# Attention and feed-forward on one core: the value products of chunks 3 to 11 in quarters of the array, in two phases

## The chip, the cores and the metric

The kernel runs on one core of one Trainium2 chip. The metric is the device time of one execution in microseconds (us), median of several runs. Engines are named as in the profile: PE is TensorE's matrix product, PEld its weight load, DVE is VectorE, ACT ScalarE, POOL GpSimd, SP SyncE, whose queue issues most transfers.

## The reference, cut to what matters

Attention over 4 batches, 8 heads, 768 positions and a head width of 64, in which each position sees the first 4 keys (sinks) and the last 128; then a feed-forward layer on 3072 rows of 512 with 2048 inner columns. All in float32.

```python
scores = scale * np.matmul(q, k.transpose(0, 1, 3, 2))
is_sink = pos[None, :] < int(n_sink)              # n_sink = 4
rel = pos[:, None] - pos[None, :]
in_window = (rel >= 0) & (rel < int(window))      # window = 128
scores = np.where(is_sink | in_window, scores, -1000000000.0)
a = np.exp(scores - np.max(scores, axis=-1, keepdims=True))
a = a / (np.sum(a, axis=-1, keepdims=True) + 1e-09)
attn_out = np.matmul(a, v)                        # (4, 8, 768, 64)
x = attn_out.transpose(0, 2, 1, 3).reshape(3072, 512)
h = x @ w_in
g = np.maximum(h, 0.0) + alpha * np.minimum(h, 0.0)
return g @ w_out
```

## The kernel before

The 3072 rows are 12 chunks of 256 queries (`QC`), three to a batch (`CPB`). A chunk's 8 heads are 4 pairs `p` (or `x`), two heads `j` each; its 256 queries are two blocks `u` of 128. A block of queries needs two blocks of 128 keys, the older and the newer one; because the window is exactly 128 wide, key place `a` (0 to 127) counts for query `b` in the older block where `a > b` and in the newer one where `b >= a`. So the softmax of the two blocks is added into one tile `comb` (L747), which is turned so that keys lie on partitions, and then multiplied by two triangular masks `tri` (128 x 2 x 128), one for each block. The first chunk of a batch (0, 3, 6, 9) has no older block for its first 128 queries.

In chunks 3 to 11 (`PAIRED` and on) a pair is turned without PE. `swap` (L830) lets DVE transpose 32 x 32 squares into `small`, SP store this to memory (`swap`, L837, one transfer) and load it back in another order (L839, one transfer) into `t`, both `comb` tiles. The masks follow at `trans` (L810): for pairs 0 and 1 `swapped` (L855, the multiplications on L863) writes both masked forms into a `wa` tile; for pairs 2 and 3 `halved` (L843, L850 and L852) writes one into a further `comb` tile and the other in place. There are 5 `comb` and 2 `wa` tiles. `masks_in_order` (L806) puts the rows of `tri` once, ahead of chunk 3, into the order in which the turned keys lie, by a store to `trid` (L807) and a load (L808); the values `v` come in the same order from an input of their own, `vq`.

`av_four` (L950) then multiplies: four full-array products with the sinks (L961) open two PSUM banks, one for pairs 0 and 1, one for pairs 2 and 3. For each pair and each block of keys `blk` follow two products, one for each head `j`, that use all 128 rows (keys) and 64 columns (head width) of the array: head 0 in the left half of the columns, head 1 in the right. Block 1 has 256 columns of queries (it is the newer block for `u` = 0 and the older for `u` = 1), blocks 0 and 2 have 128. Pairs 0 and 1 are issued in `values` (L879), pairs 2 and 3 on L977. ACT (L982) and DVE (L983) split each bank into the two parts `xh` and `xl` that the feed-forward products use: `gemm1` (L997) makes the inner columns, one block of 128 after the other, `gemm2` (L1052 to L1055) the output.

The order on every engine is written by a planner (`Plan`): each operation carries a cost, the planner draws the times from the costs and picks the next operation on every engine, and the program is issued in this order. A changed cost or buffer so moves other operations too. In the scores of chunks 0 and 1 (L675), two heads share the array by rows: 64 rows each, into two banks.

Of the kernel before, what the change touches and what calls it, by code (L numbers as in the profile page):

```python
# [9 lines left out]
F32 = mybir.dt.float32  # L10
# [7 lines left out]
ALU = mybir.AluOpType  # L18

P = 128  # L20
B, H, S, D = 4, 8, 768, 64
# [3 lines left out]
QC = 2 * P  # L25
# [3 lines left out]
CPB = S // QC  # L29
NCHUNK = B * CPB  # L30
NF = DF // P
KT = DM // P
# [56 lines left out]
class Plan:  # L89
# [20 lines left out]
    def held(self, tile_):  # L110
        v = Value(None)
        v.at = tile_
        return v

    def op(self, engine, cost, run, reads=(), writes=(), tail=0.09, mode=None, nbytes=0, other=None, locks=False):
        o = Op(engine, cost, tail, run, self.rank if engine == "PE" else None)
        o.ways = {engine: (cost, run)}
        if other:
            o.ways[other[0]] = other[1:]
        o.born = self.rank  # L120
        if engine == "PE":
# [24 lines left out]
        o.takes = [v for v in seen if v.kind]  # L146
        o.locks = locks
        self.ops.append(o)
        return o
# [161 lines left out]
def dve(n, fast=False):  # L311
    return 0.07 + (0.52e-3 if fast else 1.04e-3) * n
# [22 lines left out]
def mm(n):  # L335
    return 0.456e-3 * n
# [6 lines left out]
def native(n):  # L343
    return 1.667e-3 * n
# [3 lines left out]
ISSUE = 0.45  # L348
# [4 lines left out]
def program(ctx, tc, qk, pairs, vp, vq, vs, w, par, out):  # L353
    nc = tc.nc
# [17 lines left out]
    trid = held(scratch.tile([P, 2, P], F32, name="trid"))  # L372
# [188 lines left out]
    def known(x):  # L561
        return V.setdefault(x, held(x))
# [241 lines left out]
        op("ACT", cast(QC, True), lambda: nc.scalar.copy(st.at, tp.at[:, :QC]), reads=[tp], writes=[st])  # L804

    def masks_in_order():  # L806
        op("SP", ISSUE, lambda: nc.sync.dma_start(trid.at, tri), reads=[known("tri")], writes=[trid], nbytes=8 * P * P)  # L807
        op("SP", ISSUE, lambda: nc.sync.dma_start(tri, trid.at.rearrange("(j a) l x -> a j (l x)", j=4)), reads=[trid], writes=[known("tri")], nbytes=8 * P * P)  # L808

    def trans(c, p):  # L810
        if c in SPLIT:
# [18 lines left out]
    def swap(c, p):  # L830

        cb = comb.pop((c, p))
        small, d, t = val("comb"), val("swap"), val("comb")
        op("DVE", dve(4 * P), lambda: nc.vector.transpose(
            small.at.rearrange("p (j t b) -> p t j b", t=4, j=4), cb.at.rearrange("p (t j b) -> p t j b", t=4, j=4)),
            reads=[(cb, (j, u)) for j in range(2) for u in range(2)], writes=[small])
        op("SP", ISSUE, lambda: nc.sync.dma_start(d.at.rearrange("i (a j) x -> (i a) (j x)", j=4), small.at),  # L837
           reads=[small], writes=[d], nbytes=4 * P * 4 * P)
        op("SP", ISSUE, lambda: nc.sync.dma_start(t.at.rearrange("p (i x) -> p i x", i=4), d.at.rearrange("i p x -> p i x")),  # L839
           reads=[d], writes=[t], nbytes=4 * P * 4 * P)  # L840
        turned[c, p] = t

    def halved(c, p):  # L843

        t, e = turned.pop((c, p)), val("comb")
        at = lambda u: t.at.rearrange("p (i j u b) -> p u i j b", i=4, j=2, u=2)[:, u]
        to = lambda u: e.at.rearrange("p (j u i b) -> p u i j b", i=4, j=2, u=2)[:, u]
        mask = lambda l: tri[:, l].rearrange("p (i b) -> p i b", i=4).unsqueeze(2).broadcast_to([P, 4, 2, 32])
        for u in range(2):
            op("DVE", dve(2 * P), lambda u=u: nc.vector.tensor_tensor(to(u), at(u), mask(u), ALU.mult), reads=[t, known("tri")], writes=[(e, u)])  # L850
        for u in range(2):
            op("DVE", dve(2 * P), lambda u=u: nc.vector.tensor_tensor(at(u), at(u), mask(1 - u), ALU.mult), reads=[known("tri")], writes=[t])  # L852
        wt[c, p] = (t, e)

    def swapped(c, p):  # L855
        if p > 1:
            return halved(c, p)
        t, tt = turned.pop((c, p)), val("wa")
        full = lambda: tt.at.bitcast(F32).rearrange("p (j u l x) -> p j u l x", j=2, u=2, l=2)
        view = lambda: t.at.rearrange("p (i j u b) -> p j u i b", i=4, j=2, u=2)  # L860
        for j in range(2):
            for u in range(2):
                op("DVE", dve(2 * P), lambda j=j, u=u: nc.vector.tensor_tensor(  # L863
                    full()[:, j, u].rearrange("p l (i b) -> p l i b", i=4),
                    view()[:, j, u].unsqueeze(1).broadcast_to([P, 2, 4, 32]),
                    tri.rearrange("p l (i b) -> p l i b", i=4), ALU.mult), reads=[t, known("tri")], writes=[(tt, (j, u))])
        wt[c, p] = tt

    turned = {}

# [10 lines left out]
    def values_cost(c):  # L881
        return native(P) * (4 if c % CPB else 3)
# [31 lines left out]
    def av_split(c, g):  # L914
# [29 lines left out]
        if c and not g:  # L944
# [2 lines left out]
        op("DVE", dve(4 * P), lambda: nc.vector.tensor_tensor(x2.at[:, g], view(), x1.at[:, g].bitcast(F32), ALU.subtract),  # L947
           reads=[rb, *keys[0]], writes=keys[1])

    def av_four(c):  # L950
        every = range(KT)
        kept = [wt.pop((c, x)) for x in every]
        src = [*kept[:2], *kept[2], *kept[3]]
# [5 lines left out]
        def sinks():  # L959
# [4 lines left out]
        def all_values():  # L964
            sinks()
            for x in every:
                if x < 2:
                    values(c, v[x].at, lambda j: kept[x].at.bitcast(F32)[:, j * 4 * P:(j + 1) * 4 * P], place(x), x == 1)
                    continue
                t, e = kept[x]  # L970
                blocks = [(1, lambda j: t.at.rearrange("p (i j u b) -> p j u i b", i=4, j=2, u=2)[:, j], slice(0, 2 * P))]
                if c % CPB:
                    blocks.append((0, lambda j: e.at[:, j * QC:j * QC + P], slice(0, P)))
                blocks.append((2, lambda j: e.at[:, j * QC + P:(j + 1) * QC], slice(P, 2 * P)))
                for n, (blk, what, os) in enumerate(blocks):
                    for j in range(2):
                        nc.tensor.matmul(place(x)[j * D:(j + 1) * D, os], v[x].at[:, blk, j], what(j), start=False, stop=x == KT - 1 and n == len(blocks) - 1)  # L977
        op("PE", 4 * mm(QC) + 4 * values_cost(c), all_values, reads=src + v + [vt, st], writes=bks, tail=N_TAIL, mode="col")
# [205 lines left out]
    n = 0  # L1184
# [250 lines left out]
```

## Time and profile before

| | |
|---|---|
| median of 3 runs | 640.63 us (640.63 to 640.88) |
| profiled execution | 641.19 us, its span 639.6 us |
| PE busy | 630.7 us (99%) |
| PEld, DVE, ACT, POOL busy | 560.6, 522.0, 392.4, 35.2 us |
| granted TensorE clock | 0.999 of full speed |

A profile is of one execution, so its own time stands beside the median. The span runs from the first to the last instruction. PE's busy time joins rows that overlap: a matmul's row lasts until its results are out, while the next one starts earlier.

### The profile page before, as it was taken

The page shows a single profiled execution, that of the slowest core. Times are in us where ns is not written, and L with a number is a line of the kernel's source. Part 1 is how long each engine was busy: PE and PEld are TensorE (multiplying, and loading weights), DVE is VectorE, ACT ScalarE, POOL GpSimd, SP SyncE. Part 2 cuts the span into 40 slices and gives each one's busy share as a digit, 9 for nine tenths or more (in the row PEclk, how much of TensorE's full clock was granted, in tenths as well). Part 3 has the DMA queues.
Part 4 walks back from the last instruction along what each step waited for, and adds up shares of the span by engine and source line. Part 5 has one row for each costly group of instructions (what it writes and reads, how often), then busy time and mean ns, then how long its engine had stood idle before and what let it go on. Part 6 is the DMA issues. An engine that isn't in the chain of part 4 may idle for free. (4 is left out here: it accounts for less than half of the span.)

```text
span 639.6 us, 13100 instructions
## 1 busy us (share of the span) xinstructions
PE 630.7 (99%) x4497; PEld 560.6 (88%) x4497; DVE 522.0 (82%) x1748; ACT 392.4 (61%) x1060; POOL 35.2 (6%) x115
## 2 busy tenths in 40 slices
PE   7999999999999999999999999999999999999997
PEld 3677688979989999999989999999998998998996
DVE  6999999998969988986987997995996997895332
ACT  6998888847638636736637745654755754752332
POOL 2120000000100000000100000000100000000000
PEclk9999999999999999999999999999999999999999
DMA  8676630424344345333443344442543434421001
GB/s 315 251 261 246 240 131 22 126 82 148 110 128 151 104 124 179 92 120 109 158 133 121 128 130 130 129 136 61 165 132 112 150 100 149 130 83 35 34 3 36
DMA packets 58825, 83.08 MB, mean 130 GB/s; under 512 B 9088, under 2 KB 35328, under 8 KB 58752
## 3 DMA queue, kind: packets, MB, share of 16 engines
q1 hardware_dynamic: 55200, 69.20, 33.9%
q10 hardware_dynamic: 3552, 12.98, 5.6%
q8 instruction: 37, 0.61, 0.4%
q14 instruction: 36, 0.29, 0.1%
HBM read 65.12 MB, written 17.04 MB: 128 GB/s over the span
## 5 line engine op out<-in xcount | busy, mean ns | idle before, releaser
L1001 ACT ACTIVATE g<-bank,param 128x256 f32<-128x256 f32 x192 | 90.6, 473 | 85.9 <-PE bank L997 85.4
L997 PE MATMUL bank<-xh,win 128*128 128x256 f32 x768 | 140.0, 278 | 0.0
L997 PE MATMUL bank<-xh,w 128*128 128x256 f32 x768 | 138.9, 276 | 0.0
L997 PEld LDWEIGHTS bank<-xh,w 128*128 128x128 f32 x768 | 121.1, 192 | 1.9 <-issue 0.7
L997 PEld LDWEIGHTS bank<-xh,win 128*128 128x128 f32 x768 | 120.8, 192 | 1.8 <-issue 1.1
L1007 ACT CAST gh<-g 128x256 fp32r<-128x256 f32 x176 | 70.7, 405 | 64.5 <-DVE g L1002 63.6
L997 PE MATMUL bank<-xl,win 128*128 128x256 f32 x384 | 105.7, 275 | 0.0
L997 PE MATMUL bank<-xl,w 128*128 128x256 f32 x384 | 105.6, 275 | 0.0
L1002 DVE TENSOR_TENSOR g<-bank,g 128x256 f32<-128x256 f32 x192 | 79.9, 419 | 30.6 <-ACT g L1001 29.4
L706 ACT ACTIVATE pt<-pt,nm 128x260 f32<-128x260 f32 (+1 forms) x192 | 93.5, 488 | 16.2 <-DVE nm L700 16.1
L700 DVE CUSTOM_DVE_ANT_0 pt<-bank,masks 128x260 f32<-128x260 f32 (+1 forms) x192 | 71.2, 401 | 30.5 <-PE bank L686 21.9
L1008 DVE TENSOR_TENSOR gl<-g,gh 128x256 fp32r<-128x256 f32 x176 | 73.6, 421 | 17.1 <-ACT gh L1007 13.9
L997 PEld LDWEIGHTS bank<-xl,win 128*128 128x128 f32 x384 | 73.6, 192 | 1.7 <-issue 1.2
L997 PEld LDWEIGHTS bank<-xl,w 128*128 128x128 f32 x384 | 73.6, 192 | 1.1 <-issue 0.2
L1054 PE MATMUL bank<-w,gh 128*128 128x512 f32 x188 | 71.5, 380 | 0.0
L1055 PE MATMUL bank<-w,gh 128*128 128x512 f32 x188 | 71.3, 379 | 0.0
L1054 PE MATMUL bank<-wout,gh 128*128 128x512 f32 x160 | 60.7, 380 | 0.0
L1055 PE MATMUL bank<-wout,gh 128*128 128x512 f32 x160 | 60.6, 379 | 0.0
L646 ACT CAST kq<-stage 128x392 fp32r<-128x392 f32 (+1 forms) x80 | 39.1, 488 | 35.1 <-PE bank L686 28.0
L1052 PE MATMUL bank<-w,gl 128*128 128x512 f32 x188 | 56.4, 382 | 0.0
L1052 PE MATMUL bank<-wout,gl 128*128 128x512 f32 x160 | 47.7, 380 | 0.0
L751 POOL TENSOR_TENSOR sink<-pt,ri 128x8 f32<-128x8 f32 x80 | 20.0, 251 | 490.4 <-DVE ri L736 397.5
(150 smaller groups left out, 1098.9 us busy)
## 6 DMA issues: line engine op xcount, KB each, us to landing
stage<-qk SPq DMA_DIRECT2D x56, 324.0 KB, 2.9
wraw<-w ACTq DMA_DIRECT2D x12, 1024.0 KB, 6.2
swap<-comb SPq DMA_DIRECT2D x36, 256.0 KB, 2.0
comb<-swap SPq DMA_DIRECT2D x36, 256.0 KB, 3.2
stage<-qk SPq DMA_DIRECT2D x24, 292.0 KB, 2.9
out_dram<-ob SPq DMA_DIRECT2D x22, 256.0 KB, 2.8
v<-vq SPq DMA_DIRECT2D x24, 192.0 KB, 3.0
wraw<-w SPq DMA_DIRECT2D x4, 1024.0 KB, 9.1
```

What stands on the lines that cost most here:

```text
L646: op("ACT", cast(KC - n), lambda: nc.scalar.copy(ks()[:, :, n // 2:], k_raw()), reads=[st], writes=[(kq, "k")])
L700: o = op("DVE", dve(n), lambda: nc.vector.tensor_tensor_reduce(out=pt.at[:, u, w0], in0=s.at[:, w0], in1=masks[:, i, w0], scale=-0.125, sc ...
L706: op("ACT", exp(n), lambda: nc.scalar.activation(pt.at[:, u, w0], pt.at[:, u, w0], AF.Exp, bias=nm.at[:, h, u:u + 1], scale=-1.0, accum_ou ...
L751: op("POOL", 0.2, lambda: nc.gpsimd.tensor_tensor(sk.at[:, :, h], pt.at[:, :, P:P + NS], ri.at[:, :2].unsqueeze(2).broadcast_to([P, 2, NS] ...
L997: nc.tensor.matmul(h(), fin.win(part, ks), row, start=(kt == 0 and n == 0), stop=(kt == KT - 1 and n == 2))
L1001: op("ACT", act(QC, True), lambda: nc.scalar.activation(g.at, h(), AF.Copy, scale=alt[:, f:f + 1]), reads=[bk, known("param")], writes=[g])
L1002: op("DVE", dve(QC), lambda: nc.vector.tensor_tensor(g.at, h(), g.at, ALU.max), reads=[bk], writes=[g])
L1007: op("ACT", cast(QC), lambda: nc.scalar.copy(gh.at, g.at), reads=[g], writes=[gh])
L1008: op("DVE", dve(QC), lambda: nc.vector.tensor_tensor(gl.at, g.at, gh.at.bitcast(F32), ALU.subtract), reads=[g, gh], writes=[gl])
L1052: nc.tensor.matmul(o2[j].at, gl.at[:, js], fin.row(0), start=False, stop=(f == end))
L1054: nc.tensor.matmul(o2[j].at, gh.at[:, js], fin.row(0), start=(f == begin), stop=False)
L1055: nc.tensor.matmul(o2[j].at, gh.at[:, js], fin.row(1), start=False, stop=False)
```

## The change

Five things are edited.

- The value products (`av_four`) use 64 keys instead of 128, in the upper or lower half of the array's rows, so that a product takes a quarter of the array: rows by half `r` of the keys, columns by head `j`. Products are issued in turn over the four quarters. In the first phase the upper rows work on pairs 0 and 1 (one bank) while the lower rows work on pairs 2 and 3 (the other bank); then PE is drained; in the second phase the halves change places. In each half of the keys one of a block's two triangles is full for 64 queries and zero for the other 64, so half of the products have 64 columns ("narrow") and half 128 ("wide").
- The turned weights: the store becomes two, one for each half of the keys; the load stays one. For pairs 0 and 1 it goes to a `wa` tile instead of a `comb` tile.
- The masks: four multiplications per pair on 64 partitions each, one in place and one into a further tile (`part`; for pairs 0 and 1 the rest of the same `wa` tile).
- `masks_in_order` makes two stores and two loads, of 64 x 64 and 64 x 128 elements.
- The cost that the planner takes for the value products. The input `vq` is reordered on the host in two halves of 64 keys instead of four quarters of 32.

```diff
     def masks_in_order():
-        op("SP", ISSUE, lambda: nc.sync.dma_start(trid.at, tri), ...)
-        op("SP", ISSUE, lambda: nc.sync.dma_start(tri, trid.at.rearrange("(j a) l x -> a j (l x)", j=4)), ...)
+        for l in range(2):
+            op("SP", ISSUE, lambda l=l: nc.sync.dma_start(trid.at[:, 1 - l], tri[:D, l, :D]), ...)
+        for r in (slice(0, D), slice(D, P)):
+            op("SP", ISSUE, lambda r=r: nc.sync.dma_start(
+                tri[r].rearrange("p l x -> p (l x)")[:, :P], trid.at.rearrange("(j a) l x -> a j (l x)", j=2)), ...)
     def swap(c, p):
-        small, d, t = val("comb"), val("swap"), val("comb")
+        small, d = val("comb"), val("swap")
+        t = val("wa" if p < 2 else "comb")
...
-        op("SP", ISSUE, lambda: nc.sync.dma_start(d.at.rearrange("i (a j) x -> (i a) (j x)", j=4), small.at), ...)
-        op("SP", ISSUE, lambda: nc.sync.dma_start(t.at.rearrange("p (i x) -> p i x", i=4), d.at.rearrange("i p x -> p i x")), ...)
-        turned[c, p] = t
+        for r in range(2):
+            op("SP", ISSUE, lambda r=r: nc.sync.dma_start(
+                d.at[:, r * D:(r + 1) * D].rearrange("i (a j) x -> i a (j x)", j=2), small.at[:, r * QC:(r + 1) * QC]), ...)
+        whole = lambda: t.at.bitcast(F32)[:, :4 * P]
+        op("SP", ISSUE, lambda: nc.sync.dma_start(whole().rearrange("p (i x) -> p i x", i=4), d.at.rearrange("i p x -> p i x")), ...)
+        turned[c, p] = t, whole
-    def halved(c, p):
...
     def swapped(c, p):
...
+        t, whole = turned.pop((c, p))
+        rest = t if p < 2 else val("comb")
+        part = (lambda: t.at.bitcast(F32)[:, 4 * P:6 * P]) if p < 2 else (lambda: rest.at[:, :2 * P])
+        for r in range(2):
+            rows = slice(r * D, (r + 1) * D)
+            mixed = lambda r=r, rows=rows: whole()[rows].rearrange("p (i t b) -> p t i b", i=4, t=4)[:, :, 2 * r:2 * r + 2]
+            mask = lambda l, rows=rows: tri[rows]...
+            op("DVE", dve(2 * P), lambda ...: nc.vector.tensor_tensor(part()[rows]..., mixed(), mask(1 - r), ALU.mult), ...)
+            op("DVE", dve(2 * P), lambda ...: nc.vector.tensor_tensor(mixed(), mixed(), mask(r), ALU.mult), ...)
     def av_four(c):
...
+        low = [(1, 0, True, 0), (2, 1, True, P), (1, 1, False, P), (0, 0, False, 0)]
+        high = [(1, 1, True, P), (0, 0, True, 0), (1, 0, False, D), (2, 1, False, 3 * D)]
+        if c % CPB == 0:
+            low.pop()
+            high.pop(1)
+        def quarters(first):
+            for n in range(2):
+                for turn in range(len(low)):
+                    for r, some in enumerate((low, high)):
+                        x = 2 * (r ^ (not first)) + n
+                        blk, u, wide, to = some[turn]
+                        rows = slice(r * D, (r + 1) * D)
+                        for j in range(2):
...
+                            nc.tensor.matmul(
+                                place(x)[j * D:(j + 1) * D, to:to + (P if wide else D)], v[x].at[rows, blk, j], what,
+                                start=False, stop=not first and n == 1 and turn == len(low) - 1)
+        def all_values():
             for x in every:
                 nc.tensor.matmul(place(x), vt.at[:, x * P:(x + 1) * P], st.at..., start=x % 2 == 0, stop=False)
+            quarters(True)
+            nc.tensor.drain()
+            quarters(False)
-        op("PE", 4 * mm(QC) + 4 * values_cost(c), all_values, ...)
+        op("PE", 4 * mm(QC) + 0.5 + 4 * native(P) * (3 if c % CPB else 2.5), all_values, ...)
```

How the order moves is shown at chunk 4. On PE, the rows around its value products before the change: `bank_66` and `bank_67` are the two banks of the values, `bank_70` and `bank_71` those of the output (`gemm2`), `kq` the scores of the next chunk's heads. L961 are the sinks; "64x256" is a product over a head's 64 columns with 256 queries.

```order
L1052 MATMUL bank_71<-w_993,gl_129 128x512
L685 MATMUL bank_64<-kq_81 128x260
L686 MATMUL bank_64<-kq_81 128x260
L685 MATMUL bank_65<-kq_81 128x260
L686 MATMUL bank_65<-kq_81 128x260
L961 MATMUL bank_67<-sinkT_111,vs_112 128x256 x2
L961 MATMUL bank_66<-sinkT_111,vs_112 128x256 x2
L879 MATMUL bank_67<-wa_95,v_83 64x256 x2
L879 MATMUL bank_67<-wa_95,v_83 64x128 x4
L879 MATMUL bank_67<-wa_96,v_84 64x256 x2
L879 MATMUL bank_67<-wa_96,v_84 64x128 x4
```

The same place after the change, with the last rows ahead of the sinks (L981 now; the value products are L975):

```order
L1060 MATMUL bank_70<-w_914,gl_131 128x512
L1060 MATMUL bank_71<-w_914,gl_131 128x512
L981 MATMUL bank_67<-sinkT_111,vs_112 128x256 x2
L981 MATMUL bank_66<-sinkT_111,vs_112 128x256 x2
L975 MATMUL bank_67<-wa_95,v_83 64x128 x2
L975 MATMUL bank_66<-comb_91,v_85 64x128 x2
L975 MATMUL bank_67<-wa_95,v_83 64x128 x2
L975 MATMUL bank_66<-comb_91,v_85 64x128 x2
L975 MATMUL bank_67<-wa_95,v_83 64x64 x2
L975 MATMUL bank_66<-comb_94,v_85 64x64 x2
L975 MATMUL bank_67<-wa_95,v_83 64x64 x2
L975 MATMUL bank_66<-comb_94,v_85 64x64 x2
```

The banks now alternate from product pair to product pair. In the order before, the rows that match L1060 of `w_914` are these, and behind them stand two blocks of `gemm1` and two of `gemm2` ahead of the sinks:

```order
L1052 MATMUL bank_70<-w_913,gl_131 128x512
L1052 MATMUL bank_71<-w_913,gl_131 128x512
L997 MATMUL bank_68<-xh_116,w_1082 128x256
L997 MATMUL bank_68<-xl_118,w_1082 128x256
L997 MATMUL bank_68<-xh_116,w_1082 128x256 x2
```

So the sinks and values of chunk 4 move ahead of these 24 products of `gemm1`, 12 of `gemm2` and the 4 rows of scores. Chunks 3, 5, 7, 8, 10 and 11 move alike; in chunks 6 and 9 the place stays.

On SP, the transfers of chunk 4's pairs 1 to 3 and its sinks, before:

```order
L837 DMA swap_75<-comb_91 128x512
L839 DMA comb_92<-swap_75 128x4x128
L837 DMA swap_74<-comb_90 128x512
L792 DMA turns_76<-pt_88 128x256
L839 DMA comb_94<-swap_74 128x4x128
L794 DMA sinkT_111<-turns_76 128x4x64
L837 DMA swap_75<-comb_93 128x512
L523 DMA stage_79<-qk 128x584
L523 DMA stage_80<-qk 128x584
L839 DMA comb_90<-swap_75 128x4x128
```

And after:

```order
L842 DMA swap_75<-comb_93 4x32x256 x2
L842 DMA swap_74<-comb_92 4x32x256 x2
L846 DMA wa_96<-swap_75 128x4x128
L846 DMA comb_91<-swap_74 128x4x128
L842 DMA swap_75<-comb_90 4x32x256 x2
L792 DMA turns_76<-pt_89 128x256
L846 DMA comb_93<-swap_75 128x4x128
L794 DMA sinkT_111<-turns_76 128x4x64
L523 DMA stage_79<-qk 128x584
L523 DMA stage_80<-qk 128x584
```

Each store is two transfers; pair 2's stores now stand ahead of pair 1's load, and pair 3's load ahead of the next chunk's two inputs (`stage`).

## Rows read from the trace of the kernel before

**Rows 1.** The page: span, and busy time of the engines.
```profile
span 639.6 us, 13100 instructions
PE 630.7 (99%) x4497; PEld 560.6 (88%) x4497; DVE 522.0 (82%) x1748; ACT 392.4 (61%) x1060; POOL 35.2 (6%) x115
```

**Rows 2.** Windows: busy time of each engine in one stretch.
```profile
core 0: us, PE busy (x) PEld busy (x) DVE busy (x) ACT busy (x) POOL busy (x), PEclk, DMA share, GB/s
188.06:634.90 446.84, 446.84 (x3283) 415.30 (x3282) 350.19 (x1252) 249.40 (x709) 18.88 (x66) 1.00 0.36 112
```

**Rows 3.** Waits of PE, longest and shortest: us in total, times, longest us.
```profile
PE bank L801 <- DVE ts L783: 1.7, 2, 0.9
...
PE bank L821 <- DVE wa L825: 0.2, 1, 0.2
```

**Rows 4.** Timeline of PE, chunks 3 and 4: start us, us, instructions.
```profile
188.63 1.52 PE L879 MATMUL bank<-wa,v 128*64 128x256 f32 x16
...
191.38 0.70 PE L1052 MATMUL bank<-wout,gl 128*128 128x512 f32 x2
...
232.38 0.27 PE L997 MATMUL bank<-xh,w 128*128 128x256 f32 x1
...
238.09 0.64 PE L961 MATMUL bank<-sinkT,vs 128*128 128x256 f32 x4
238.66 1.96 PE L879 MATMUL bank<-wa,v 128*64 128x256 f32 x24
240.45 1.91 PE L977 MATMUL bank<-comb,v 128*64 128x256 f32 x24
...
242.29 0.38 PE L685 MATMUL bank<-kq 128*128 128x260 f32 x1
```

**Rows 5.** Windows, L879 alone: PE and PEld busy (x) within 0.02 us.
```profile
188.62:188.64 0.02, 0.01 (x2) 0.02 (x2) 1.00 0.00 0
```

**Rows 6.** Windows of L675 alone (PE, PEld), and its timeline on PE.
```profile
22.49:22.52 0.03, 0.02 (x2) 0.02 (x2) 1.00 0.40 137
...
22.50 0.71 PE L675 MATMUL bank<-stage 64*128 64x260 f32 x4
```

**Rows 7.** Lines L879 and L977: ns min/median/max, first and last start.
```profile
L879 PE MATMUL bank<-wa,v x240: 272/273/431, 132.8 to 588.0; 128*64 128x128 f32 x76, 128*64 128x256 f32 x44
...
L977 PEld LDWEIGHTS bank<-comb,v x192: 137/137/137, 189.9 to 589.6; 128*64 128x64 f32 x192
L977 PE MATMUL bank<-comb,v x192: 272/273/379, 190.0 to 589.7; 128*64 128x128 f32 x120, 128*64 128x256 f32 x72
L977 PEldq EVENT_SEMAPHORE  x18: 51/51/51, 188.6 to 587.6; - x18
```

**Rows 8.** Tile tri: its multiplications and its load, columns as above.
```profile
L863 DVE TENSOR_TENSOR wa<-comb,tri x72: 381/415/424, 167.2 to 574.1; 128x256 f32<-128x256 f32 x72
L850 DVE TENSOR_TENSOR comb<-comb,tri x36: 415/419/427, 182.3 to 582.1; 128x256 f32<-128x256 f32 x36
...
L808 SPq DMA_DIRECT2D tri<-trid x1: 590/590/590, 139.1 to 139.1; - x1
```

**Rows 9.** Line L837, SP's issues of the store, columns as above.
```profile
L837 SPq DMA_DIRECT2D swap<-comb x36: 319/326/698, 158.4 to 576.7; - x36
```

**Rows 10.** Timelines of PE and DVE: last scores of chunk 4; chunk 6.
```profile
219.13 0.27 PE L686 MATMUL bank<-kq 128*128 128x260 f32 x1
...
319.20 0.28 PE L686 MATMUL bank<-kq 128*128 128x260 f32 x1
...
331.01 0.76 DVE L852 TENSOR_TENSOR comb<-comb,tri 128x256 f32<-128x256 f32 x2
...
333.02 0.44 PE L879 MATMUL bank<-wa,v 128*64 128x256 f32 x2
```

**Rows 11.** Timeline of ACT at chunk 3: the two copies of the banks.
```profile
190.19 0.59 ACT L982 CAST xh<-bank 128x512 fp32r<-128x512 f32 x1 [2.46 <-PE bank L879]
191.49 0.59 ACT L982 CAST xh<-bank 128x512 fp32r<-128x512 f32 x1 [0.71 <-PE bank L977]
```

More of the change, by code (lines that the diff above doesn't have):

```diff
@@ L371, in program @@
     plan.kind("turns", [scratch.tile([4, P, 2 * 32], F32, name=f"turns{i}") for i in range(2)])
-    trid = held(scratch.tile([P, 2, P], F32, name="trid"))
+    trid = held(scratch.tile([D, 2, D], F32, name="trid"))
     several("stage", 2, [P, QC + KC], F32)
@@ L806, in masks_in_order @@
     def masks_in_order():
[L807 to L808 removed]
+        for l in range(2):
+            op("SP", ISSUE, lambda l=l: nc.sync.dma_start(trid.at[:, 1 - l], tri[:D, l, :D]), reads=[known("tri")], writes=[(trid, l)], nbytes=4 * D * D)
+        for r in (slice(0, D), slice(D, P)):
+            op("SP", ISSUE, lambda r=r: nc.sync.dma_start(
+                tri[r].rearrange("p l x -> p (l x)")[:, :P], trid.at.rearrange("(j a) l x -> a j (l x)", j=2)), reads=[trid], writes=[known("tri")], nbytes=8 * D * D)
     def trans(c, p):
@@ L836, in swap @@
             reads=[(cb, (j, u)) for j in range(2) for u in range(2)], writes=[small])
-        op("SP", ISSUE, lambda: nc.sync.dma_start(d.at.rearrange("i (a j) x -> (i a) (j x)", j=4), small.at),
-           reads=[small], writes=[d], nbytes=4 * P * 4 * P)
-        op("SP", ISSUE, lambda: nc.sync.dma_start(t.at.rearrange("p (i x) -> p i x", i=4), d.at.rearrange("i p x -> p i x")),
-           reads=[d], writes=[t], nbytes=4 * P * 4 * P)
-        turned[c, p] = t
-    def halved(c, p):
[L845 to L853, printed above, removed]
@@ L855, in swapped @@
-    def swapped(c, p):
[L856 to L867, printed above, removed]
+        for r in range(2):
+            op("SP", ISSUE, lambda r=r: nc.sync.dma_start(
+                d.at[:, r * D:(r + 1) * D].rearrange("i (a j) x -> i a (j x)", j=2), small.at[:, r * QC:(r + 1) * QC]),
+               reads=[small], writes=[(d, r)], nbytes=2 * P * 4 * P)
@@ new lines, in swap @@
+        whole = lambda: t.at.bitcast(F32)[:, :4 * P]
+        op("SP", ISSUE, lambda: nc.sync.dma_start(whole().rearrange("p (i x) -> p i x", i=4), d.at.rearrange("i p x -> p i x")),
+           reads=[d], writes=[t], nbytes=4 * P * 4 * P)
+        turned[c, p] = t, whole
+    def swapped(c, p):
+        t, whole = turned.pop((c, p))
[4 more added lines that the diff above has]
+            mixed = lambda r=r, rows=rows: whole()[rows].rearrange("p (i t b) -> p t i b", i=4, t=4)[:, :, 2 * r:2 * r + 2]
+            mask = lambda l, rows=rows: tri[rows].rearrange("p l x -> p (l x)")[:, l * D:(l + 1) * D].rearrange("p (i b) -> p i b", i=2).unsqueeze(1).broadcast_to([D, 4, 2, 32])
+            op("DVE", dve(2 * P), lambda r=r, rows=rows, mixed=mixed, mask=mask: nc.vector.tensor_tensor(
+                part()[rows].rearrange("p (t i b) -> p t i b", t=4, i=2), mixed(), mask(1 - r), ALU.mult),
+               reads=[(t, r), known("tri")], writes=[(rest, ("rest", r))])
+            op("DVE", dve(2 * P), lambda r=r, mixed=mixed, mask=mask: nc.vector.tensor_tensor(mixed(), mixed(), mask(r), ALU.mult),
+               reads=[known("tri")], writes=[(t, r)])
+        wt[c, p] = [t] if p < 2 else [t, rest], whole, part
@@ L948, in av_split @@
            reads=[rb, *keys[0]], writes=keys[1])
+    halfway = nc.alloc_semaphore("halfway")
     def av_four(c):
@@ L952, in av_four @@
         kept = [wt.pop((c, x)) for x in every]
-        src = [*kept[:2], *kept[2], *kept[3]]
+        src = [t for k in kept for t in k[0]]
         v = [vtile.pop((c, x)) for x in every]
@@ L957, in av_four @@
         place = lambda x: bks[x // 2].at[:, x % 2 * QC:(x % 2 + 1) * QC]
-        def sinks():
+        low = [(1, 0, True, 0), (2, 1, True, P), (1, 1, False, P), (0, 0, False, 0)]
[11 more added lines that the diff above has]
+                        for j in range(2):
+                            if wide:
+                                what = kept[x][1]()[rows].rearrange("p (i t b) -> p t i b", i=4, t=4)[:, 2 * j + u]
+                            else:
+                                what = kept[x][2]()[rows, (2 * j + u) * D:(2 * j + u + 1) * D]
+                            nc.tensor.matmul(
+                                place(x)[j * D:(j + 1) * D, to:to + (P if wide else D)], v[x].at[rows, blk, j], what,
+                                start=False, stop=not first and n == 1 and turn == len(low) - 1)
@@ L960, in sinks @@
+        def all_values():
             for x in every:
                 nc.tensor.matmul(place(x), vt.at[:, x * P:(x + 1) * P], st.at.rearrange("p (i u b) -> p u i b", u=2, i=4), start=x % 2 == 0, stop=False)
+            quarters(True)
+            nc.tensor.drain()
+            quarters(False)
         x1, x2 = begin_x(c, 0)
[L964 to L977, printed above, removed]
@@ L978, in av_four @@
-        op("PE", 4 * mm(QC) + 4 * values_cost(c), all_values, reads=src + v + [vt, st], writes=bks, tail=N_TAIL, mode="col")
+        op("PE", 4 * mm(QC) + 0.5 + 4 * native(P) * (3 if c % CPB else 2.5), all_values, reads=src + v + [vt, st], writes=bks, tail=N_TAIL, mode="col")
         for n, bk in enumerate(bks):
@@ L1420 @@
         'vp': vp.reshape(NCHUNK, KT, P, 6 * D),
-        'vq': np.ascontiguousarray(vp.reshape(NCHUNK, KT, 4, P // 4, 6 * D).swapaxes(2, 3)).reshape(NCHUNK, KT, P, 6 * D),
+        'vq': np.ascontiguousarray(vp.reshape(NCHUNK, KT, 2, 2, D // 2, 6 * D).swapaxes(3, 4)).reshape(NCHUNK, KT, P, 6 * D),
         'vs': rows,
```

## The prediction, made before the changed kernel ran

> **What bounds the kernel now.** The page says that the span is 639.6 us and that TensorE (PE) is busy for 630.7 us of it, 99% [rows 1]. A busy share alone is not a bound, so the next view is busy time in one stretch, from the first product of chunk 3's values (188.06) to the end of the matrix products (634.90): PE is busy for 446.84 us of 446.84, at a granted clock of 1.00, while VectorE (DVE) has 350 and ScalarE (ACT) 249 [rows 2]. All nine places that the change touches lie in this stretch. In the list of waits PE has seven entries, from 1.7 us down to 0.2, and none of them names a line of the value products [rows 3]. So PE is the bound, with a queue of work that does not run dry there, and a microsecond saved on PE ends the kernel a microsecond earlier, unless an operand comes late.
>
> What PE does at the place is read from its timeline. Chunk 4: the sink products from 238.09, the value products from 238.66, the next line's product at 242.29: 3.63 us for the values. Chunk 3, which is the first of its batch and has no older block of keys: 188.63 to 191.38, 2.75 us [rows 4]. In the trace a float32 matmul is two rows, so chunk 4's 24 matmuls are 48 rows (24 of L879, 24 of L977 [rows 4]). The two heads of a pair sit in the two column halves of the array and run at once: within 0.02 us two matmul rows and two weight loads start [rows 5]. So each half streams 4 pairs x 512 columns x 2 rows = 4096 columns in chunk 4, and 4 x 384 x 2 = 3072 in chunk 3. The two stretches give the price of a column, (3.63 - 2.75) / 1024 = 0.86 ns, and a fixed part of 2.75 - 3072 x 0.86 ns = 0.11 us for entering and leaving the mode.
>
> **The value products in quarters (a gain).** With 64 keys to a product, that part of a triangle which is all zero falls away: a pair needs 128 + 128 + 64 + 64 = 384 columns in each half of the keys where it needed 512, and in chunks 3, 6 and 9 it needs 320 in one half and 256 in the other. If four quarters run at once, each streams 2 phases x 2 pairs x 384 x 2 rows = 3072 columns: 3072 x 0.86 ns + 0.11 = 2.75 us without the drain. In chunks 3, 6 and 9 the longer quarter sets it: 2 x 2 x 320 x 2 = 2560 columns, 2.31 us.
>
> Do four quarters run at once? No row of before shows four. Column halves do [rows 5]. Row halves do as well: the scores of chunk 1 (L675) put two heads into 64 rows each, and there too two loads and two matmuls start within 0.03 us, and the four rows of 260 columns end within 0.71 us [rows 6]; one after the other they would stream 4 x 260 x 0.86 ns = 0.89 us, before loads and the last one's tail. Those two heads write to different banks, as the two key halves of one phase do. The bounds are four at once and two at once (a rival below). I take four: each halving is shown at the full rate, and I see nothing in the rows that all four would have to share.
>
> **The drain (a loss).** PE has no drain between products in this trace, so it is bounded. Below: the tail of the last matmul. The shortest rows, those of 128 columns, last 272 ns [rows 7], but the next one starts after 128 x 0.86 = 110, so 0.16 us of it is hidden now and is not then. Above: with a whole weight load (137 ns) and a semaphore instruction of PE's queue (51 ns) behind it [rows 7], 0.35. I take 0.26: the tail, the semaphore's 0.05, and 0.05 for the part of a load that shows, which is how far the longest row of L879, the first after the sinks, is over the longest of L977 (431 against 379 [rows 7]). Chunks with three blocks: 2.75 + 0.26 = 3.01, a gain of 0.62. Chunks 3, 6, 9: 2.31 + 0.26 = 2.57, a gain of 0.18.
>
> **More and shorter rows.** Chunk 4 goes from 24 matmuls to 64, so from 48 + 48 rows (loads and products) to 128 + 128. At the full rate one must start every 2.64 us / 256 = 10 ns. Bursts are faster (four starts in 0.02 us [rows 5]); nothing in before asks for it over a longer time. I put it at nothing and keep it as a rival.
>
> **The masks (nothing).** Four multiplications a pair before, four after, on 64 partitions instead of 128 but with 256 elements on each as before: about 0.42 us as now [rows 8].
>
> **Two stores and one load.** Each of 36 pairs issues one more store, 0.33 us of SyncE's (SP's) queue [rows 9]. Behind it in that queue stand the load of the same pair and the next chunk's inputs; the turned weights land about 0.33 us later, and what could be late next are the masks of the last pair, then the values. At the same time the order puts the values earlier: in chunk 4 ahead of the two blocks of the first matrix product and two of the second that now take PE from 232.38 to 238.09 [rows 4]. From the last scores of chunk 4 to its first value product PE has 238.66 - 219.13 = 19.5 us now. But chunk 6, whose place stays, has only 333.02 - 319.20 = 13.8 even now; its last masks end at 331.77, and PE did not wait [rows 10]. That is 1.25 us of cover, of which 0.33 goes. The other seven chunks get chunk 6's distance, and with the first two pairs' loads in another buffer the later pairs' stores are issued before the earlier loads. So nothing is lost; with the cover gone, a microsecond of lateness would cost seven.
>
> **Both banks close at the end.** Now ACT copies the first bank at 190.19, in the midst of the values, and the second at 191.49 [rows 11]. After the change both are complete only with the last phase, so both copies (1.2 us) come behind the values, the last some 0.6 us later against their end. Cover: what PE does next are products of the chunk before and scores (L1052, L685 [rows 4]), and the new chunk's own first product stands two blocks further off than before. Nothing.
>
> **Reordering the masks once** takes 2 + 2 small transfers for 1 + 1. The second pair is issued at 139.1, for masks first used at 167.2 [rows 8]: nothing. The first pair costs at most one issue of 0.33 us in the loading phase.
>
> **Sum.** 6 x 0.62 + 3 x 0.18 = 4.3 us. The profiled execution took 641.19 us (1.6 around its span of 639.6), 0.56 over the median of 640.63: 636.9 against its own time, 636.4 against the median. With the drain at 0.16 or 0.35 the latter is 635.5 or 637.2, and 0.3 more if the start loses.
>
> **Rivals.**
> *Two at a time, slower.* If the two key halves take turns, for an input or a result path that they share, a chunk of three blocks streams 6144 columns one after the other: 5.28 + 0.37 = 5.65 us, 2.02 more than now; chunks 3, 6, 9 stream 2560 + 2048: 4.33, 1.58 more. Together +16.9: 657.5. It turns on the overlap: 4.3 us of gain against 6 x 2.64 + 3 x 2.20 = 22.4 us of streaming, so from 19% over the full rate on the change loses. Against it stand rows 5 and 6, for it that no row has four. A queue of PE's that cannot start a row every 12.7 ns ((3.63 - 0.37) / 256) over a whole phase ends on the same side, and I count it here.
>
> *A least distance between products, no change.* If matmul rows cannot start closer than some distance, whichever quarter they go to, a three-block chunk is even at (3.63 - 0.37) / 128 = 25 ns; chunks 3, 6, 9 with 96 rows then take 2.77 and lose 0.02. About 0 in all: 640.6. Against it stand the two starts within 0.02 us [rows 5]; for it, that the whole stretch of chunk 4 has one start in 76 ns (3.63 / 48), so that no row tests it for long. The Trainium skill, "TensorE: Matmul & The Clock Gate", section "Wait — 56ns, not 53.3ns?", says that start-to-start never drops below about 25 ns however small the product is; by that rule the change is worth nothing, and rows 5 disagree with it for two halves of the array.
>
> *In between.* Rows of 64 columns (55 ns) do not quite cover their weight loads: 10% over the full rate takes back 2.2 us, 638.6.
>
> *Operands late.* 0.6 us of waiting in seven chunks takes the gain back: 640.6.
>
> **How the numbers follow.** Full rate 62%, in between 12%, least distance 8%, operands late 5%, two at a time or bound by the queue 13%. The likeliest gives 636.4. The range runs from 635.2 (the drain at its lower bound, and 0.3 less) to 641.0, just past the two cases without change: it leaves out the 13% and a few at the edges. 0.2% (1.3 us) is about what a measurement of this kernel can tell from no change. Faster: 62 + 12 + 1 = 75%. Same: 8 + 2 = 10%. Slower: 13 + 2 = 15%.
>
> **What would show it.** Right: the values of chunk 4 take 3.0 us from the first product to the next line, those of chunk 3 2.6; four matmul rows start within some 0.03 us; the phases stand 0.26 us apart; PE waits for no mask and no load. Wrong: the rows of the two key halves alternate, starts keep a fixed distance, or PE stands idle ahead of the first quarter.

## The result, and the profile after

The changed kernel takes 649.48 us (median of 4 runs, 648.53 to 650.08) against 640.63 us: 1.0136 of the time before, 95% interval 1.0119 to 1.0154. I had forecast 636.4, and a range up to 641.0. One execution of those reported further down, of the old kernel with two slow stores, ran at a granted clock of 0.59 and took 1027.54 us; it is left out of that run's ratio, and its trace is not used. The profiled execution of the changed kernel took 648.53 us. Its page and its windows, from the first sink product of chunk 3 to the end of the matrix products (columns as in [rows 2]):

```profile
span 647.0 us, 14516 instructions
...
PE 629.9 (97%) x5167; PEld 562.0 (87%) x5169; DVE 531.8 (82%) x1748; ACT 392.4 (61%) x1060; POOL 33.1 (5%) x115
```
```profile
184.45:642.30 457.85, 450.84 (x3989) 420.94 (x3989) 364.28 (x1265) 251.81 (x716) 18.27 (x66) 1.00 0.37 111
```

PE, which had no idle time in that stretch [rows 2], is now idle for 457.85 - 450.84 = 7.0 us of it: 5.5 ahead of the sinks of the later chunks, 0.9 in the nine drains, and 0.7 behind the last product, which ends at 641.63. Ahead of the stretch it stands for another 1.8 before chunk 3's sinks. The granted clock is 1.00 as before, so a slower array is not the reason. PE's list of waits has a new first entry beside those of [rows 3]:

```profile
PE bank L981 <- DMA sinkT<-turns: 7.2, 8, 1.9
PE bank L801 <- DVE ts L783: 1.3, 2, 0.8
```

L981 are the sink products, the first that a chunk's values ask for. PE's timeline at chunk 4, which answers to [rows 4]:

```profile
233.22 0.59 PE L1060 MATMUL bank<-w,gl 128*128 128x512 f32 x2
234.11 0.74 PE L981 MATMUL bank<-sinkT,vs 128*128 128x256 f32 x4 [0.29 <-DMA sinkT<-turns]
234.78 0.33 PE L975 MATMUL bank<-wa,v 64*64 64x128 f32 x2
234.79 0.33 PE L975 MATMUL bank<-comb,v 64*64 64x128 f32 x2
...
236.13 0.70 PE L975 MATMUL bank<-comb,v 64*64 64x64 f32 x6
236.52 0.33 PE L975 MATMUL bank<-wa,v 64*64 64x128 f32 x2
...
238.00 0.38 PE L1005 MATMUL bank<-xh,w 128*128 128x256 f32 x1
```

Two things are to be seen. The values take 238.00 - 234.78 = 3.22 us, against 3.63 before: the quarters do gain. And PE stands ahead of the sinks. Summed over nine chunks, the first sink product starts 7.1 us behind the recorded end of the row ahead of it, where it started 1.5 us ahead of that end before: 8.6 us later. The sinks themselves, now behind a pause, take 0.85 us more; the values take 2.6 us less. That is 6.9 of the 7.4 us between the spans; 0.5 is spread over the rest.

Why the sinks are late is seen in SP's queue at the last pair of chunk 3 and its sinks. Before:

```profile
174.18 0.32 SPq L837 DMA_DIRECT2D swap<-comb  x1
175.13 0.32 SPq L792 DMA_DIRECT2D turns<-pt  x1
176.18 0.37 SPq L839 DMA_DIRECT2D comb<-swap  x1
176.88 0.37 SPq L794 DMA_DIRECT2D sinkT<-turns  x1
```
```profile
SPq L839 <- DMA swap<-comb: 27.6, 22, 2.1
```

And after:

```profile
175.45 1.08 SPq L842 DMA_DIRECT2D swap<-comb  x2
176.63 0.42 SPq L792 DMA_DIRECT2D turns<-pt  x1
180.96 0.36 SPq L846 DMA_DIRECT2D comb<-swap  x1
181.38 0.50 SPq L794 DMA_DIRECT2D sinkT<-turns  x1
```
```profile
SPq L846 <- DMA swap<-comb: 96.0, 36, 4.4
```

The two stores of a pair (L842) cost SP 1.08 us, not 2 x 0.33 [rows 9]. The pair's load (L846) waits until 180.96, 5.5 us behind the first store's issue in place of 2.0, and the sinks' load (L794) stands behind it in the queue. SP waits 96.0 us for these stores in 36 waits; before it was 27.6 us in 22. The masks of the last pair are late too: on DVE the rows at chunk 4 are

```profile
233.70 0.87 DVE L859 TENSOR_TENSOR comb<-comb,tri 64x256 f32<-64x256 f32 x2 [1.28 <-DMA comb<-swap]
234.60 0.87 DVE L862 TENSOR_TENSOR comb<-comb,tri 64x256 f32<-64x256 f32 x2
```

and they end at 235.47, when the sinks have already run. Before, the last masks ended 0.7 to 2.6 us ahead of the first sink product.

### The profile page after: what moved, and what is told of

It is laid out like the page before. It is cut to its first block, busy times and chain, and to the rows that moved or that the text cites. A ratio compares the mean times of both kernels' runs of the same rounds, so it can differ in the third digit from the quotient of the medians.

```text
span 647.0 us, 14516 instructions
## 1 busy us (share of the span) xinstructions
PE 629.9 (97%) x5167; PEld 562.0 (87%) x5169; DVE 531.8 (82%) x1748; ACT 392.4 (61%) x1060; POOL 33.1 (5%) x115
## 4 chain that ended last, share of the span: by engine, by line
PE 59%; DVE 20%; DMA 11%; ACT 4%; issue 3%; SPq 1%; POOL 0%; ACTq 0%; DVEq 0%; POOLq 0%
PE bank L1005 25%; PE bank L1062 7%; PE bank L1063 7%; PE bank L1060 7%; DMA swap<-comb 5%; PE bank L975 4%; DMA sinkT<-turns 4%; DVE g L1010 2%; DVE pt L700 2%; PE bank L685 2%; PE bank L686 2%; DVE comb L838 2%; DVE gl L1016 2%; DVE comb L747 2%; PE bank L1051 2%
## 5 line engine op out<-in xcount | busy, mean ns | idle before, releaser
L1060 PE MATMUL bank<-w,gl 128*128 128x512 f32 x188 | 56.0, 379 | 0.0
L1060 PE MATMUL bank<-wout,gl 128*128 128x512 f32 x160 | 47.6, 379 | 0.0
L648 DVE TENSOR_TENSOR kq<-stage,kq 64x392 fp32r<-64x392 f32 (+1 forms) x80 | 42.7, 534 | 3.2 <-ACT kq L646 0.7
```

Of the source, the lines that this page charges most:

```text
L648: op("DVE", dve(KC - n), lambda: nc.vector.tensor_tensor(ks()[D:, :, n // 2:], k_raw()[D:], ks()[D:, :, n // 2:].bitcast(F32), ALU.subtrac ...
L1060: nc.tensor.matmul(o2[j].at, gl.at[:, js], fin.row(0), start=False, stop=(f == end))
```

## The experiments

Each run is compared with the kernel before on the same chip (medians of 640.48 to 640.57 us); the ratio to it and its 95% interval stand behind the time. "Landing" below is worked out from the trace: from a pair's store's issue (the first of the two, where there are two) to the end of the last packet of the store's size that starts ahead of the pair's load, median over the 36 pairs. A neighbour's packets of the same size can fall into it, so it is good to some 0.2 us.

**Another form of the stores.** The diff holds a form that I had not weighed: the new stores go to `d.at[:, r * D:(r + 1) * D]` as "i a (j x)", half of each `i`, so `i` and `a` can't be merged, and a store is 4 outermost x 32 pieces of 1 KB. The store of before was 128 pieces in one row. First, the scratch half by half, so that each of the two stores is 128 pieces again:

```diff
-scratch.tile([4, P, P], F32, name=f"swap{i}")
+scratch.tile([2, 4, D, P], F32, name=f"swap{i}")
-    d.at[:, r * D:(r + 1) * D].rearrange("i (a j) x -> i a (j x)", j=2), small.at[:, r * QC:(r + 1) * QC])
+    d.at[r].rearrange("i (a j) x -> (i a) (j x)", j=2), small.at[:, r * QC:(r + 1) * QC])
-nc.sync.dma_start(whole()..., d.at...)
+for r in range(2): nc.sync.dma_start(whole()[r * D:(r + 1) * D]..., d.at[r]...)
```

> The changed kernel, with its scratch laid out half by half: the same two stores of a pair, but each as 128 pieces of 1 KB along one dimension (as the one store of before was) in place of 4 x 32 pieces; the load becomes two of 64 partitions. Theory A (the form of the store, 4 outermost, lands late, and SP's queue holds the last pair's load and the sinks' load behind it): a store is issued in 0.33 us instead of 0.52, its pair's load follows some 2 to 2.5 us behind it instead of 5, PE no longer stands ahead of the sinks (8.6 us in nine chunks now, below 2 then), and the time is 639 to 641, against 649.5 of the changed kernel. Rival B (only the order: the planner puts the values too early): PE still stands some 8 us ahead of the sinks, 648 to 650. Rival C (the number of transfers: one store more in SP's queue): with four transfers a pair in place of three it gets no better, 649 to 651. Rival D (the quarters themselves are slow): 648 or more with no gap ahead of the sinks.

Measured: 638.12 us, 0.996 (0.9946 to 0.9974). Landing 1.83 us, against 4.90 in the changed kernel and 1.66 before. No gap ahead of any of the nine sinks. From the first issue to the end of the second the two stores keep SP for 0.80 us in the median, 1.02 at chunk 3's last pair, against 1.08 in the changed kernel, so the issue is the small part of what came back.

The same scratch with one store of 128 x 2 pieces and two loads:

```diff
-for r in range(2): nc.sync.dma_start(d.at[r]..., small.at[:, r * QC:(r + 1) * QC])
+nc.sync.dma_start(d.at.rearrange("r i (a j) x -> (i a) r (j x)", j=2), small.at.rearrange("p (r y) -> p r y", r=2))
```

> The changed kernel with the half by half scratch, and one store of a pair of 128 x 2 pieces of 1 KB in place of two of 4 x 32 pieces, and two loads: three transfers a pair as in the changed kernel. Theory A: as with two flat stores, 638.5 to 640.5, PE stands below 2 us ahead of the sinks in all. Rival B: 648 to 650. Rival C (number of stores): this one recovers, 639 to 641, and the two flat stores do not. Rival D: 648 or more with no gap ahead of the sinks.

Measured: 637.61 us, 0.9953 (0.9939 to 0.9966), the fastest of all. Landing 1.80 us. The first of PE's waits, and chunk 4 there:

```profile
PE bank L801 <- DVE ts L783: 1.3, 2, 0.8
PE bank L1236 <- DVE fm L627: 1.2, 1, 1.2
```
```profile
231.53 0.59 PE L1061 MATMUL bank<-w,gl 128*128 128x512 f32 x2
231.96 0.65 PE L982 MATMUL bank<-sinkT,vs 128*128 128x256 f32 x4
232.54 0.33 PE L976 MATMUL bank<-wa,v 64*64 64x128 f32 x2
...
235.71 0.38 PE L1006 MATMUL bank<-xh,w 128*128 128x256 f32 x1
```

The wait for the sinks is gone, and the values take 3.18 us (2.70 in chunks 3, 6, 9). Both runs speak for theory A: rivals B (order) and D (quarters) would have stayed at 648, and C (number) falls with the two flat stores, which have one transfer more than the changed kernel. The planner gave these two kernels an order of their own, so the form is tested once more below with the order held.

**The old kernel with two stores.** Meant as the slow form, alone, in the old order:

```diff
-nc.sync.dma_start(d.at.rearrange("i (a j) x -> (i a) (j x)", j=4), small.at)
+for r in range(2):
+    nc.sync.dma_start(d.at.rearrange("i (a j) x -> i a (j x)", j=4)[:, :, r * QC:(r + 1) * QC], small.at[:, r * QC:(r + 1) * QC])
```

> The kernel before, with nothing changed but its one store of a pair: split into two of 4 x 32 pieces of 1 KB, the form of the changed kernel. No quarters, no drain, old masks. Theory A: the store lands some 3 us later, chunks 6 and 9, whose sinks' load is issued only 4 us ahead of the sinks, lose 2 to 3 us each and the others (10 to 12 us ahead) little: 643 to 647, and a wait of PE for the sinks' load appears. Rivals B and D (order or quarters alone): 640.6 within 0.5. Rival C: as A, some us slower.

Measured: 640.53 us, 1.000 (0.9991 to 1.0009). But the form was not the slow one: here `i` and `a` lie in one even step, so the stores are 128 pieces in one row, and in the trace they land at 1.95 us. So this run says only that one store more, in the fast form, costs nothing in the old kernel (rival C), and nothing on the form.

**The planner told of it.** `tail=2.6` on the changed kernel's stores, so that the order expects them later.

> The changed kernel, its transfers as they are, but the planner is told that a store's data land 2.6 us later than it assumed. Only the order changes. Theory A with B (both are needed: late data, and an order that does not know of it): the values of chunks are put later behind other matrix products, PE stands 1 to 3 us ahead of the sinks in all instead of 8.6, 640 to 643. If the order cannot make room (SP's queue itself is the limit): 646 to 649. Rival D: 648 or more.

Measured: 639.45 us, 0.9982 (0.9973 to 0.9991). The stores still land at 4.92 us, but no gap is left ahead of the sinks. What is late next are masks:

```profile
PE bank L975 <- DVE comb L862: 1.7, 2, 1.2
```

The values of chunks 6, 9 and 10 take 3.46, 4.19 and 3.66 us, 2.7 us more together than in the kernel with one store. (The traced execution took 640.47 us, the longest of the eleven.) So lateness and an order that does not know of it make the loss together.

**The slow form in the old order**, now with a gap in the scratch that keeps `i` and `a` apart; the order of PE, DVE and ACT is instruction by instruction that of the run with two fast stores:

```diff
-scratch.tile([4, P, P], F32, name=f"swap{i}")
+scratch.tile([4, 2 * P, P], F32, name=f"swap{i}")
+    d.at[:, :P].rearrange("i (a j) x -> i a (j x)", j=4)[:, :, r * QC:(r + 1) * QC], small.at[:, r * QC:(r + 1) * QC])
```

> The kernel before (full-width value products, old masks, old order), its one store of a pair made into two with 4 outermost x 32 pieces of 1 KB: a gap in the scratch keeps the 4 from being merged into 128. The earlier run on the kernel before, with two stores of 128 pieces, was no test of the form. Theory A (form and order together): the stores take 0.52 us of SP each and the load follows some 5 us behind; the old order leaves 10 to 12 us between the sinks' load and the sinks in seven chunks, so these lose nothing; chunks 6 and 9, with 4 us, lose 0 to 2.5 each: 640.5 to 645, and where PE stands at all it is ahead of the sinks of chunks 6 and 9. Rival (the form alone costs, whatever the order): 646 to 650, a gap ahead of the sinks of all nine. Rival (the form costs nothing): stores of 0.33 us, loads 2 us behind, 640.5.

Measured: 650.22 us, 1.0141 (1.0126 to 1.0157); the trace is of a second series of the same kernel.

> The kernel before with two stores of 4 x 32 pieces once more, for a profile at full clock: 648.5 to 651.6 as before. If the late landing is what costs, PE's list of waits names the sinks' load or the masks ahead of the sinks and value products, some 9 us in all, and SP's queue waits some 4 us for each store ahead of its load. If instead the loss is spread over the matrix products (a lower granted clock, or transfers of inputs that come late behind SP's waits), the sinks start without a gap and PE's waits name inputs or nothing.

Measured: 649.74 us, 1.0145 (1.013 to 1.0161). The place was right, the size was not, and PE's waits come to 5.6 us where I had expected some 9:

```profile
PE bank L963 <- DMA sinkT<-turns: 4.7, 2, 2.4
...
PE bank L979 <- DVE comb L854: 0.9, 1, 0.9
```

PE stands 2.3 and 2.4 us ahead of the sinks of chunks 6 and 9 and of no others. But in chunk 3 a mask comes late in the midst of the values (0.9 us), and behind the pause of chunk 9 the granted clock falls, as its windows show:

```profile
480.00:487.50 7.50, 5.33 (x37) 4.66 (x35) 5.41 (x15) 2.10 (x6) 0.00 (x0) 1.00 0.46 118
487.50:493.00 5.50, 5.30 (x38) 3.88 (x39) 3.33 (x10) 1.17 (x3) 0.00 (x0) 0.69 0.45 153
493.00:500.00 7.00, 7.00 (x54) 6.68 (x53) 3.83 (x11) 3.42 (x9) 0.00 (x0) 1.00 0.23 77
```

PE is idle for 2.2 of the first 7.5 us, and in the next 5.5 the mean granted clock is 0.69, part of it at 1.2 GHz and the rest at 2.4: the sinks take 0.90 us instead of 0.57, the values 4.10 instead of 2.75. Behind the pause of chunk 6, as long, the clock did not fall: 0.64 and 2.75. Of the 8.8 us between this span and that of the run with two fast stores, 5.0 are the two gaps, 1.7 the slower sinks and values of chunk 9 and 1.2 the values of chunk 3; the rest is spread. Landing 4.85 us.

One such store instead of two, 4 x 32 pieces of 2 KB (`small.at` whole): the kernel before with nothing changed but this instruction's form, and the gap in the scratch that makes it.

> The kernel before with its one store of a pair in another form and nothing else: 4 outermost x 32 pieces of 2 KB, kept apart by a gap in the scratch, in place of 128 pieces. The number of stores, their bytes, the pieces and the order of every engine are those of before. The run with two such stores took 650.2 where two stores of 128 pieces took 640.5, so the form alone costs in the old order too, which I had not expected. If the store's landing goes by 4 outermost: the same bytes over the same few DMA engines, so it lands as late as the two did: 647 to 651, and PE stands ahead of the sinks in chunks 6 and 9 above all. If the two stores' issue (2 x 0.52 us of SP) made half of the loss: 643 to 647. If only the 1 KB pieces together with the form are slow: 640.5 to 642.

Measured: 674.80 us, 1.0514 (1.0491 to 1.0537). All my figures were too low. The place shows best what the form does: DMA share in tenths and GB/s of the same store of chunk 3, first in the kernel before (174.1 to 177.5 us, slices of 0.085 us), then here (175.0 to 181.4, slices of 0.16):

```profile
DMA  0000000000499999995101799851000000000455
GB/s 0 0 0 0 0 0 0 0 0 0 169 361 386 386 386 386 386 386 217 24 0 60 253 349 373 313 169 24 0 0 0 0 0 0 0 0 30 126 151 145
```
```profile
DMA  9951000025400901124177986422222222110000
GB/s 352 320 160 32 0 0 0 13 64 51 26 0 0 45 0 13 6 58 77 58 122 166 250 250 179 135 102 102 102 102 90 102 102 90 70 51 32 0 0 0
```

Before, the DMA engines are busy for over nine tenths and move 386 GB/s, and the store is through in nine slices. Here the store is left alone in the later slices: a share of two tenths, 102 GB/s. It lands at 5.81 us. How many engines a store uses can be counted, too: behind its data the trace has packets of 4 bytes, 16 for a store before, 4 for one here. Over the run that is 36 x 12 = 432 small packets less, as the two pages show, first before, then here:

```profile
DMA packets 58825, 83.08 MB, mean 130 GB/s; under 512 B 9088, under 2 KB 35328, under 8 KB 58752
```
```profile
DMA packets 58393, 83.08 MB, mean 123 GB/s; under 512 B 8656, under 2 KB 34896, under 8 KB 58320
```

The gap by itself is not what costs: the load that reads it has its last packet 2.4 us behind its issue, against 2.7 before. PE waits for masks and sinks:

```profile
PE bank L977 <- DVE comb L852: 12.2, 7, 3.4
PE bank L961 <- DMA sinkT<-turns: 7.1, 2, 3.6
```

and with the pauses the mean granted clock is 0.981. Over a span of 676 us that would be some 13 us, an upper estimate from that mean, since PE loses nothing by a low clock while it stands.

**The slow form in the kernel with two flat stores**: a gap in its scratch too (`[2, 4, P, P]`, `d.at[r][:, :D]`), the same order on PE, DVE and ACT.

> The kernel with two flat stores (638.1), with a gap in its scratch so that each store is again 4 outermost x 32 pieces of 1 KB: nothing else differs, and the order of PE, VectorE and ScalarE is the same instruction by instruction. If the form of the store is the whole of the loss: the changed kernel's time, 648 to 651, with PE standing 7 to 10 us ahead of the sinks. If its order was part of it, or the one load in place of two: 641 to 646. If the two loads (64 partitions each) were what mended it: 638.

Measured: 669.70 us, 1.0457 (1.0431 to 1.0483), 31.6 us over the same kernel without the gap.

```profile
PE bank L983 <- DMA sinkT<-turns: 17.0, 9, 3.4
```

With the order held, the form makes the loss here too, and a larger one than in the changed kernel. There one load follows, here two of 64 partitions, and together they take 1.97 us of SP's queue ahead of the next stores in chunk 3. Whether that is the whole of the further 20 us was not tried apart.

**The price of a drain.** One drain more in the middle of each phase of the kernel with one store, 18 in all. The drain that is there already, between the phases of chunk 4, in the kernel with one store:

```profile
233.87 0.23 PE L976 MATMUL bank<-wa,v 64*64 64x64 f32 x2
233.88 0.66 PE L976 MATMUL bank<-comb,v 64*64 64x64 f32 x4
234.23 0.33 PE L976 MATMUL bank<-wa,v 64*64 64x128 f32 x2
```

The second row joins two products ahead of the drain and, from 234.21 on, two behind it.

> The kernel with one store of 128 x 2 pieces (637.6), with one more drain in the middle of each phase, 18 in all: the price of a drain. From the rows a drain adds 0.25 to 0.29 us between the starts of two products, and the weight load behind it is not hidden, 0.05: 18 x 0.25 to 0.34 = 4.5 to 6.1 us, 642.1 to 643.7. If a drain only costs once, when the banks change hands: below 639.

Measured: 644.62 us, 7.0 over 637.61: 0.39 us for each, a little over the expected 0.25 to 0.34. On the timeline a drain puts 0.29 us between the starts of two products beyond their usual distance, and the first row behind it takes 0.05 longer to the next; of the rest, most goes with the first extra drain, behind which the four quarters run out of step (their starts, within 0.02 us before, spread over 0.13).

**The planner's cost of the values corrected** to 3.76 and 3.28 us, in the kernel with one store.

> The kernel with one store of 128 x 2 pieces (637.6), with the planner's cost of the sinks and value products set to what the trace of that kernel shows (3.76 us, and 3.28 in chunks 3, 6, 9, in place of 3.53 and 3.10). PE waits nowhere in that stretch, so only the order can move: 637.2 to 638.0, no difference that can be measured.

Measured: 637.91 us, 0.996 (0.9946 to 0.9973): no difference to 637.61 that can be measured, as expected.

A kernel without the drain was not tried: in its place two halves of the rows would add into one bank at the same time.

## Why the prediction was wrong, by its own steps

- **PE is the bound**: right for before, and right again as soon as the stores are fast. The loss is PE standing, the sign of being wrong that the prediction names last, and 0.1 us more in the sinks behind each pause.
- **"Two stores and one load"**: this step failed. It took the price of a store from [rows 9], 0.33 us of SP's queue and the same landing, and put that the turned weights land 0.33 us later, against 1.25 us of cover, "so nothing is lost". But the row is of a store of 128 pieces in one dimension, and the new one has 4 outermost, as the list of transfers ahead of the prediction already had it (4x32x256 for 128x512). Each costs 0.52 us of SP, and the pair lands 4.90 us after the first issue in place of 1.66: 3.2 us late, over twice the cover. That the moved order gives the other chunks about chunk 6's distance was seen rightly, and so was that without cover every chunk pays for itself: 8.6 us in nine, 0.95 on average, from 0.05 to 2.1. The rival "operands late" had the mechanism, with 0.6 us and a chance of 5%. Two pairs of runs, each with one order, show that the form is enough: 640.53 against 649.74 (old kernel, two stores), 638.12 against 669.70. And with the order told of the late landing, 639.45, most of the loss goes though the form stays.
- **The form and the engines.** In the trace the packets of a pair's stores, their times added up and divided by the stretch from the first to the last, are 13.3 at a time before, 4.1 in the changed kernel, 4.1 and 3.6 in the old one with two and one slow stores. The packets of 4 bytes say the same, 16 against 4 for a store; in the two pairs of runs with 72 stores the pages count 864 = 72 x 12 small packets less with the slow form (8800 for 9664, 9536 for 10400). The Trainium skill, "DMA: Bandwidth & Descriptors", section "Why a DMA increments its semaphore by 16 and not by 1", says that a transfer uses the largest number of engines up to 16 that divides the outermost size of both its sides, and on a queue like SP's the lowest-numbered ones: 16 for 128, 4 for 4, and the same four for both stores of a pair. The trace agrees on the number, with 386 against 102 GB/s; which engines they were it does not show. At these two rates a pair's 256 KB take 0.7 and 2.6 us, as an estimate 1.9 us more, past the cover of 1.25, so reading the new access pattern for its outermost size would have turned the forecast. The packets are slower as well (those of 2 KB took 127 ns each in the one slow store, 86 before); why was not tried.
- **Four quarters at the full rate**: right. The rows of wide products follow at 0.109 us in every quarter, and the four start within 0.02 us. The least distance does not hold: a phase of chunk 4 starts 64 rows in 1.39 us, 22 ns on average and 7 ns within a group of four. The rule of about 25 ns that the prediction cited from the Trainium skill ("TensorE: Matmul & The Clock Gate", section "Wait — 56ns, not 53.3ns?") is so not borne out across quarters; the measurement decides.
- **The gain of a chunk, mis-sized**: 0.62 and 0.18 us forecast, 0.45 and 0.05 measured where no operand is late (3.18 and 2.70 us for the values). Of the 0.17 that is missing in chunk 4, 0.08 is the drain (0.29 more than the usual 0.06 between starts, and 0.05 for the first product behind it: 0.34 in place of 0.26, at the upper bound of 0.35), 0.04 the rows (the 16 narrow ones of a quarter follow at 58 ns in place of 55), and 0.06 entering and leaving: 0.05 more than usual behind the first row and 0.12 behind the last, in place of the 0.11 estimated. The sum, 6 x 0.45 + 3 x 0.05 = 2.85 us in place of 4.3, is what the kernel with one store shows: 640.51 - 637.61 = 2.9.
- **Masks**: right, 0.42 us each in the median, as before. **Both banks closing at the end** and **the reordering of masks**: nothing seen; with fast stores no wait of PE names them.

## What to carry to other kernels

The price of a transfer belongs to its form: before a row's duration is taken over for a new transfer, compare both sides' outermost sizes, and ask whether slicing has kept two dimensions from merging. Splitting a transfer whose landing other transfers of the same queue wait behind is to be priced by its landing, not by its issue: two flat stores kept SP for 0.80 us, two slow ones for 1.1, but landed 3 us earlier and lost nothing. Where a planner sets the order, a wrong landing time turns into waits of the bound engine, since it moves the consumer up to where the data should have been.

## What the runs showed that I had not expected

One instruction's form, with the same bytes and pieces, took the old kernel from 640.5 to 674.8 us, while two stores of half the size in that form took it to 649.7: both use few engines, but one such store lands at 5.8 us and the pair at 4.9. Why one store lands later than two is open. Pauses can cost more than themselves: the sinks took 0.57 us without a pause and 0.64 to 0.68 behind most pauses, and behind one pause of 2.4 us the mean granted clock was 0.69 for 5.5 us, while behind another of 2.3 us in the same run it did not fall. A drain in the midst of a phase cost 0.39 us, more than the 0.34 of one between phases; behind the first of the two in chunk 4 the quarters lost their step.
